# A conformer layer on one core: a new order of the blocks on all five engines and new PSUM banks, with the same instructions

## The chip, the core and the metric

The kernel runs on one core of a Trainium2 chip. A core has five engines, each with a queue of its own that it works off in order: PE (TensorE, matmuls; its weight loads are shown apart as PEld), ACT (ScalarE), DVE (VectorE), POOL (GpSimd) and SP (SyncE, which here issues DMAs). They meet at semaphores. The metric is device time in microseconds (us) of one execution, the median of the runs.

## The reference, cut to what matters

The input is 2 sequences of 4,000 tokens with 144 features, in bf16; there are 4 heads of 36 features and a convolution of 5 taps.

```python
h = _layernorm(x); x = x + 0.5 * (_silu(h @ w_ff1a) @ w_ff1b)          # 144 -> 576 -> 144
h = _layernorm(x); q, k, v = heads(h @ w_qkv)
p = _softmax(einsum('bhqd,bhkd->bhqk', q, k) * Dh ** -0.5)              # 4000 x 4000 per head
x = x + einsum('bhqk,bhkd->bhqd', p, v) @ w_o
h = _layernorm(x) @ w_pw1; h = a * _sigmoid(b)                          # a, b: its halves
c = sum(hp[:, i:i + T] * dw[i] for i in range(5)); x = x + _silu(c) @ w_pw2
h = _layernorm(x); x = x + 0.5 * (_silu(h @ w_ff2a) @ w_ff2b)
return _layernorm(x)
```

## The kernel before

Work is cut into 16 chunks of 500 tokens, 8 for each sequence (`NCH`, `CPB`, `CH`). For each chunk the first feed-forward and the projections come first (`ff1`, L1323, `pre2`, L1364; the first chunk in halves, `pre_first`, L1330), then attention, then `post1` (L1464: output projection WO, gated unit) and `post2` (L1588: convolution, second feed-forward, last normalisation, store).

Attention dominates. For a chunk of queries the keys are taken in 62 tiles of 64 and one rest of 32. Each tile gives scores of 4 heads on a 2 x 2 split of the PE array: four matmuls PS<-QT,KT of 64 x 500 (`emit_S`, L1742). The exponential goes one of two ways: on ACT, one instruction PT<-PS of 128 x 1000 over two banks (`emit_exp`, L1756), or on DVE, by four kinds of instruction on the bits of the number (`dve_tile`, L1770). Then come the products with V, PS<-PT,VA, four matmuls of 37 x 500 a tile (`o_quads`, L1806). The 37th row is the sum for the softmax. When a chunk's keys are done, `epilogue` (L1668) copies the sums out of the accumulators (QT<-PS; the QT buffer is used again for this), transposes them on PE (PS<-IDF,QT), takes reciprocals (RD) on DVE and multiplies (AN). The V products accumulate in banks 6 and 7; all other matmuls share banks 0 to 5.

Normalisations (`ln`, L1068) are statistics on DVE (ST), a power on POOL (RS), and the scaled rows XN on POOL (on DVE or ACT at the start and the end). Their transposes go through DRAM: a transpose of 32 x 32 blocks on DVE (`STREAM_TRANSPOSE`), four writes rows<-XN issued by SP, and two reads XT<-rows or XTQ<-rows (`blocks`, L994); the attention output takes the same way as AN. SP works in order: a read that waits for its writes to land holds what is behind it. Silu in the middle of the run is made from tanh (TH on ACT, then HT, U or SW on DVE), since exp and tanh need no reload of ACT's function table; at the end, behind the last exp, one table load (L2061) brings in Silu itself.

The order of the program has two layers. A scheduler (`Sched`, `pick`) records all operations once in an order that its estimated costs suggest, in blocks (steps). Then `reorder` (L279) moves the blocks of each engine by a table written out by hand or by a tool, `ORDER` (L38: "pe" from L39, "act" L70, "dve" L83, "pool" L102, "sp" L106). Each character is one block of that engine; P means stay, the characters before and behind it in `ALPHABET` (L37) mean one, two, ... places earlier or later. `PLACES` (L111) has one digit for each of the 1,724 PSUM tiles: the bank where it lies (`place`, L257); a tile of two banks takes the next one too. Both tables are only data. Dependences are kept: `reorder` finds anew which earlier tile of a bank has to be read out before a tile is written, sets the first and the last matmul of each accumulation by the new order, and `finish` (L344) works out semaphores and waits for it. `replay` (L388) emits the instructions, all from one line, L398, so the profile shows nearly everything under that line and the names of the tiles tell what it is.

Of the kernel before, what the change touches and what calls it, by code (L numbers as in the profile page):

```python
# [39 lines left out]
        "PPPPPPQOQOPPPPPRPNPPQQQQLPPQORPNPRPTMORNNVO~OLNOMrMMNPMMNNNOMNNNOPLMQMMMNNPMMNSMNLMMOOPNSOMQMSPNOPU["  # L40
        "OMNRMOPPQIRMSNPNePNOOOcNNNNNNNNNOOLbNLOOQNSH]MMOLOMPMMOOOVPNOOOOPPPTOOOTPMUQMSLNNQQNQOQQNPPPPPTPPROK"
        "PPPPPPPPPPPP`PPPQKVPPKPPMPPRPUPPPROQQQRZOQQQRRKQRRSJPRRRRRRRWSZRNYUR~NHQ@R[KEGOOOPPPPKQOPPSPPSLPQMTP"
        "PPLQQQMPPPQVPPQOX_PTOPPCRTQQRGSQIQQSQRNV8OOQNNVSNOOLOPUUNN_MMWLNNRMMMMOOOPPPPPPQQNPPRSNRSSSORRVTR[OR"
        "AKQ@PPLOOQQNPPPPPUOOOOOPQOPPPPPUOOOOQRPLU`NNNXMMPNLQMNLZRNL`MN_YLLMK`KMNLILNQJMOOOPNYOPNOOOQNNZ^NNNN"
        "OOPNQNQOYP]CNNNNOMPMSO[NKOOQNVMPMMN`NbYMMMMNOMNIcLLNL[MMMNNQNRMJQLLROQSPLRNOQOPUQOMPQMPPRPVPLQOMQNPQ"
        "QQQSKPQSQKQQQQJPPPPPWQQSPKKQQUPPPSWPQRPQAVPPPQCVPQRPWHSYPHSOPQYPQEPQCPRZUPPSOOHDPR^OKOOOOPNOOOO^NOQN"
        "NOOOSNNNNS[NNNdRMNRKYNJWJNNNNNNGOOPP^YNNNNOMNNNNRNNPPPVROOLOOPPRZNNOOOOOPNOSOPNRPSMOOPQOQWNRPRLLNSZP"
        "NPQOIOQOTPPPRPQ]P^USPMMQIQKQQ8QTQQGMRRTQQKRRRRGLRSOMRPQQQJQQRPVP[OOOQEROO^IOQLNOOPPTTOMNQ[FOQNPPSPPM"
        "HPQOQQUPLOPNVPNOOSQNLUOOPNOXPPPLTQNLMPPPQOPPTOOPTPLOOQRNOPPPQOVPNOOOORZOP[PPMOOFRZOL[ROQKQTUBOKNFPPP"
        "_OOOOOOPNOOOOWNNVNNXMNTKMNOMZQOSLNOMSPSLLTPMOOUOPNOOTQOMOPPPQOPPPQOPPPTTQOSQSSSSNEEPQOPTPTMOMORSNNOP"  # L50
        "ROYPQOPQ^NPNPQOPAOOOOOSOOOPPPQQNPPPPPPXOOOOOOOaNPPPLOOOPUMOOOO[IOOPSOOQNPHPSWOOPPPPQGPPPPQQQMPPQQNPQ"
# [12 lines left out]
        "_MORR_NPP^OHCNNNOZOWL~NHLMMNNNSOOXNOQQNSSOIVKPNPN]NOOOOOPPVOOOITNPPLPPQOWPPMRPNTKOOTNOPUMOOOQN`OOOPN"
        "OOPPPLOZOQQMPIQO^YROQQRLENO_PNPPPTQNNOROOSVO]QMNRNOPWTNOMNSOPQXbOOOQ[NO~NCdIMMMMMMMfbKMMMQMMJLMPLMUM"
        "MMNL^TR^JSLJQJUKPNLHQMPP`UNNNNOMOOOOPNOOPPPPQQNPQQQMUQQMSOPTQOPTPQUNQSPSQ<TRSSVEQQQHQQFPPPPPQSPMYTOL"
        "NNTMNNNP^[NOMNNQMMOLNN]PNOOR[OPKQN_ZLNESMOOKHOM[NPPLPNOOPPMQSTMNPQQQQRSQRRTCQVNGRNOMTTTMMNUPPQHNQSPM"
        "YVTQKLLSSOIJPSSPTMKORNOQOPPPPPPSORNSMRNRRRNQQRPFRPQQQQQQRPFQO"
    ),
    "act": (  # L70
        "PPPPPPPPPPPPPRSNNOSOOOPPPPPPPUPNOXNNOOOOOQNPPPPPPPPPROOPPQOPPPQOPPPPPPQQNPPPPPPPPPPPPPPPPPPPPPPPPPQO"
        "PPPPPPPPPPPPPPPPPPPPPPPPPPPPPPPPPPPPPPPPPPPPPPPPPPPPPPPPPPPPPPPPPPPPPPPPQOROSNOOPPPPPPPPPPPPPPPPPPPP"
        "PPPPPPPPPPPPPQOPPPPPPPPPPPPPPPPPPPPPPPPPQOPPQOPPPPPPPPPPPPPPPPPPPPPPPPPPPPPPPPPPPPPPPPPPPPPPPPPPPPPP"
        "PPPPPPPPPPPPPPPPPPPPPPPPPPPPPPPPPPPPPPPPPPPPPPPPPPPPPPPPPPPPPPPPPPPPPPPPPPPPPPPPPPPPPQOPPPPPPPPPPPPP"
        "PPPPPPPPPPPPPPPPPPPPPPPPPPPPPPQOPPQOPPPPPPPPPPPPPPPPPPPPPPPPPPPPPPPPPPPPPPPPPPPPROOPPQOPPPPPPPPPPPPP"
        "PPPPPPPPPPPPPPPPPPQOPPPPPPPPPPPPPPPPPPPPPPPPPQOQOPPPPPPPPPPPPPPPPPPPPPPPPPPPPPPPPPPPPPPPPPPPPPPPPPPP"
        "PPPPPPPPTOPNOPPPPPPPPPPPPPPPPPPPPPPPPPPPPPPPPPPPPPPPPPPPPPPPPPPPPPPPPPPQOPPPPQOPPPPPPPPPPPPPPPPPPPPP"
        "PPPPPPPPPPPPPPPPPPPPPPPPPPPPPPPPPPPPPPPROOPPQQNPPPPPPPPPPPPPPPPPPQOPPPPPPPQOPPPPPPPPPPPPPPPPPPPPPPPP"
        "PPPPPQOPPPPPPPPPPPPPPPPPROOPPPPPPPPPPPPPPPPPQOPPPPPPPPPPPPQOPPPPPPPPPPPPPPPPPPPPPPPPPPPPPPPPPPPPPPPP"
        "PQOPPPPPPPPPPPPQOPPPPPPPPPPPPPPPPPPPPPPPPPPPPPPPPPPPPPPPPPPPPPPPPPPPPPPPPPPQOPPPPPPPPPPPPPPPPPPPPPPP"  # L80
        "PPPPPPPPPPPPPPPPPPPPPPPPPPPPPPPPPQOSPNRNOQOUQNPMOPPPRORNQNPPPPPPQOROQQMPPPPPPQOPPPWORNNNOO"
    ),
# [2023 lines left out]
```

## Time and profile before

| | us |
|---|---|
| median of 3 runs | 881.04 (880.92 to 881.92) |
| span of the profiled execution | 880.5 |
| PE busy | 851.5 |
| ACT busy | 849.6 |
| DVE busy | 822.7 |
| POOL busy | 300.4 |

The profile is of one execution, taken by the hardware profiler; its own time is its span, 880.5 us, and the granted clock of TensorE is 1.00 nearly throughout. In the groups, out<-in names tiles, partitions x elements and type; then come count, busy us, mean ns of one, and after the bar the idle time of the engine just before, with what ended it. Matmuls overlap, and their ends are modelled, so a busy PE is not a PE at its peak. In a timeline, a row is start, length, engine, operation and count; in brackets stands the idle time before it and who ended it. SPq rows are DMA issues of SP.

### The profile page before, as it was taken

To read this page: it belongs to the slowest core of one execution; us is meant where nothing else is said; L and a number is where in the kernel's file an instruction comes from. 1 tells how busy PE (TensorE), PEld (TensorE's weight loads), DVE (VectorE), ACT (ScalarE), POOL (GpSimd) and SP (SyncE) were. 2 spreads that over 40 slices of the span, in tenths; PEclk is the share of its full clock that TensorE was granted. 3 is DMA by queue.
4 is the path that set the end of the run, shared out by engine and by line. 5 is a ranking of instruction groups with operands and counts; after the bars stand their busy time and mean duration, and the time that the engine had idled before them with its cause. 6 is when DMAs were issued, how large, how long until landed. Compare 5 with 4: busy or idle time off the path is not lost.

```text
span 880.5 us, 27000 instructions
## 1 busy us (share of the span) xinstructions
PE 851.5 (97%) x11419; PEld 380.2 (43%) x11419; DVE 822.7 (93%) x1812; ACT 849.6 (96%) x1098; POOL 300.4 (34%) x584
## 2 busy tenths in 40 slices
PE   8998999999999999999999999999999999999996
PEld 6543433344444443443444444344443433444366
DVE  7977999999999999999989999899999999999987
ACT  6799999999999999999999999999999999999986
POOL 7770331431336130252111813522513404032434
PEclk9999999999999999999999999999999999999999
DMA  3221001220221110212001120110110011001111
GB/s 100 44 55 38 16 18 36 62 51 16 40 49 38 23 38 22 45 24 45 16 9 30 36 44 23 23 26 20 43 31 18 21 37 20 17 12 36 27 27 33
DMA packets 114351, 28.80 MB, mean 33 GB/s; under 512 B 101090, under 2 KB 114230, under 8 KB 114230
## 3 DMA queue, kind: packets, MB, share of 16 engines
q1 hardware_dynamic: 112646, 26.39, 13.8%
q8 instruction: 89, 1.46, 0.7%
q10 hardware_dynamic: 1584, 0.69, 0.3%
q14 instruction: 32, 0.26, 0.1%
HBM read 13.44 MB, written 13.61 MB: 31 GB/s over the span
## 4 chain that ended last, share of the span: by engine, by line
ACT 46%; PE 33%; DVE 17%; POOL 2%; DMA 1%; issue 1%; SPq 1%; POOLq 0%; DVEq 0%
ACT PT L398 42%; PE PS L398 33%; DVE PT L398 7%; ACT TH L398 4%; DVE HT L398 2%; DVE ST L398 2%; DVE X L398 2%; DVE XN L398 2%; POOL RS L398 1%; POOL XN L398 1%; DVE KT L398 1%; DVE QT L398 1%; DVE AN L398 1%; SPq L398 1%; DMA rows<-XN 0%
## 5 line engine op out<-in xcount | busy, mean ns | idle before, releaser
L398 ACT ACTIVATE PT<-PS 128x1000 bf16<-128x1000 f32 (+1 forms) x818 | 757.2, 1074 | 4.1 <-PE PS L398 2.4
L398 PE MATMUL PS<-QT,KT 64*64 64x500 bf16 x3968 | 425.7, 385 | 13.0 <-ACT PT L398 5.2
L398 PE MATMUL PS<-PT,VA 64*37 64x500 bf16 x4728 | 411.5, 372 | 1.8 <-DVE QT L398 0.7
L398 DVE TENSOR_SCALAR PT<-PS 128x500 int16<-128x500 f32 x380 | 250.1, 668 | 5.8 <-PE PS L398 3.9
L398 PEld LDWEIGHTS PS<-QT,KT 64*64 64x64 bf16 x3968 | 123.4, 104 | 236.8 <-ACT PT L398 137.1
L398 POOL TENSOR_SCALAR RS<-ST 125x4 f32<-125x4 f32 x130 | 37.0, 284 | 482.2 <-DVE ST L398 475.6
L398 PEld LDWEIGHTS PS<-PT,VA 64*37 64x37 bf16 x4728 | 141.4, 96 | 96.2 <-DVE PT L398 18.7
L398 DVE TENSOR_SCALAR PT<-PT 128x1000 uint16<-128x1000 uint16 x380 | 154.5, 418 | 2.1 <-PE PS L398 0.8
L398 POOL TENSOR_SCALAR XN<-X,RS 125x144 bf16<-125x144 bf16 x260 | 150.4, 610 | 13.1 <-DMA out_dram<-XN 6.4
L398 DVE TENSOR_TENSOR PT<-PT 128x1000 bf16<-128x1000 bf16 x190 | 128.8, 679 | 1.3
L398 ACT ACTIVATE TH<-PS 128x500 bf16<-128x500 f32 (+3 forms) x194 | 107.3, 575 | 7.4 <-PE PS L398 6.5
L398 POOL TENSOR_TENSOR RS<-RS,NHALF 125x4 f32<-125x4 f32 (+1 forms) x93 | 91.7, 989 | 33.1 <-DVE RS L398 27.3
L398 DVE SCALAR_TENSOR_TENSOR HT<-TH,PS 128x500 bf16<-128x500 bf16 (+1 forms) x135 | 81.2, 615 | 12.8 <-ACT TH L398 12.0
L398 PE MATMUL PS<-XT,WA 80*128 80x500 bf16 (+5 forms) x288 | 74.5, 365 | 2.2 <-DMA XT<-rows 0.9
L398 DVE BATCH_NORM_STATS2 ST<-X 125x6 f32<-125x288 bf16 x160 | 65.7, 447 | 2.8 <-DMA X<-in_x_dram 2.7
L398 DVE SCALAR_TENSOR_TENSOR X<-PS,X 125x288 bf16<-125x288 f32 (+1 forms) x128 | 56.6, 449 | 6.5 <-PE PS L398 5.2
L398 PE MATMUL PS<-WB,HT 128*125 128x144 bf16 (+1 forms) x640 | 52.4, 230 | 0.7 <-ACT HT L398 0.5
L398 PEld LDWEIGHTS PS<-WB,HT 128*125 128x125 bf16 (+1 forms) x640 | 44.3, 136 | 14.5 <-issue 3.8
L398 PEld LDWEIGHTS PS<-XT,WA 128*128 128x128 bf16 (+1 forms) x288 | 21.2, 97 | 38.8 <-issue 10.6
L398 PE MATMUL PS<-U,DG 128*128 128x250 bf16 (+6 forms) x204 | 29.6, 264 | 0.0
L398 DVE STREAM_TRANSPOSE XN<-XN 128x320 f32<-128x320 f32 x54 | 27.0, 500 | 1.0 <-POOL XN L398 1.0
L398 POOL COPY U<-U 128x2 bf16<-128x2 bf16 (+1 forms) x54 | 9.2, 209 | 46.3 <-DVE U L398 46.3
(95 smaller groups left out, 522.6 us busy)
## 6 DMA issues: line engine op xcount, KB each, us to landing
rows<-XN SPq DMA_DIRECT2D x216, 40.0 KB, 2.0
XT<-rows SPq DMA_DIRECT2D x56, 128.0 KB, 2.0
rows<-AN SPq DMA_DIRECT2D x60, 40.0 KB, 2.0
X<-in_x_dram SPq DMA_DIRECT2D x15, 140.6 KB
XTQ<-rows SPq DMA_DIRECT2D x26, 70.3 KB
out_dram<-XN SPq DMA_DIRECT2D x13, 140.6 KB
XT<-rows SPq DMA_DIRECT2D x56, 16.0 KB, 1.9
out_dram<-XN SPq DMA_DIRECT2D x3, 70.3 KB
```

The source lines that it names most:

```text
L398: ins = getattr(eng, o.name)(*o.a, **o.k)
```

## The change

The two tables are replaced; no other line differs. Of the tables' characters:

```diff
 ORDER = {
     "pe": (
-        "PPPPPPQOQOPPPPPRPNPPQQQQLPPQORPNPRPTMORNNVO~OLNOMrMMNPMMNNNOMNNNOPLMQMMMNNPMMNSMNLMMOOPNSOMQMSPNOPU["
+        "PPPPPPPPQOPPPPQSPMOPQSQOLPQQNUOPQOLZOROMNVNuMQLxLJNSMMNNKNNNNNPQLNUJMMNOKLQRVLLILMOQOKOPPPSSPMMPTfOM"
...
     "sp": (
-        "PPPPPPPPQOPPPPPPPPPPPPPPSOTNNOOPPPQOPPPROQNPPPPPPPPPPPPPQOPPQOQOPPPPPPPPPPPPPPQOPPPPPVOPNSNNQMPPPQOP"
+        "PPPPPPPPPPPPPPPPPPPPPPPPRPRMOPPPQOPTOOOOPQOPPPPPQOPPPPPPQOPPPPPPPPPPQOQOPPPPPPQOPPPPPQOQOROOSOOOPQOP"
...
 PLACES = (
-    "4540352315301235404310523035204320244354321123203214052534114030254011540241204124012410314032034023"
+    "5103152514010310254310523035213500204345323420103501230352145130422410351241204124012410314032034023"
...
```

Counted in the two programs' orders, engine by engine (a block is what the tables move):

| engine | blocks | blocks in another place | mean shift, places | largest |
|---|---|---|---|---|
| PE | 2,855 | 2,230 | 2.6 | 26 |
| ACT | 1,093 | 125 | 0.15 | 4 |
| DVE | 1,680 | 946 | 1.05 | 17 |
| POOL | 130 | 67 | 1.2 | 12 |
| SP | 157 | 80 | 0.8 | 9 |

193 of the 1,724 PSUM tiles get another bank, 46 of them among the first 86 and 57 among the last 86.

150 lines of the change are left out of this document (75 added, 75 removed).

## The prediction, made before the changed kernel was run

> **What bounds the kernel now.** I read the page first: span, busy line and chain.
>
> ```profile
> span 880.5 us, 27000 instructions
> PE 851.5 (97%) x11419; PEld 380.2 (43%) x11419; DVE 822.7 (93%) x1812; ACT 849.6 (96%) x1098; POOL 300.4 (34%) x584
> ACT 46%; PE 33%; DVE 17%; POOL 2%; DMA 1%; issue 1%; SPq 1%; POOLq 0%; DVEq 0%
> ```
>
> Three engines are nearly full at once, and the chain passes between them. ACT is the one without choice: its instructions stay what they are, so 849.6 us is a floor, and a new order can save at most the 30.9 us in which ACT is idle. Where that idle time lies is the next view, busy time by stretch (columns: stretch, length, then busy us and count of PE, PEld, DVE, ACT, POOL; granted clock, DMA share, GB/s).
>
> ```profile
> 22.00:44.00 22.00, 20.03 (x207) 11.67 (x207) 21.02 (x55) 16.15 (x30) 16.89 (x34) 1.00 0.21 44
> 44.00:110.00 66.00, 63.28 (x868) 26.13 (x867) 53.98 (x114) 64.15 (x80) 23.23 (x44) 1.00 0.17 37
> 110.00:286.00 176.00, 172.90 (x2378) 71.72 (x2379) 171.49 (x371) 173.71 (x210) 61.47 (x113) 1.00 0.18 39
> 286.00:836.00 550.00, 538.93 (x7308) 227.50 (x7304) 523.31 (x1094) 548.38 (x680) 166.85 (x321) 1.00 0.13 27
> 836.00:858.00 22.00, 22.00 (x260) 14.21 (x257) 19.26 (x52) 19.75 (x39) 6.74 (x18) 1.00 0.13 29
> 858.00:880.50 22.50, 15.85 (x195) 13.85 (x193) 17.79 (x70) 13.56 (x35) 9.61 (x13) 0.93 0.11 33
> ```
>
> From 286 to 836 us ACT is idle 1.62 us of 550: there an order can lose, and hardly win. The rest is in the front (5.85, 1.85 and 2.29 us idle in the first three stretches) and in the end (2.25 and 8.94). From 22 to 44 it is DVE that is full (0.98 us idle). The third view is who waited for whom (us in total, times, longest).
>
> ```profile
> PEld PS L398 <- ACT PT L398: 148.3, 406, 1.1
> ACT TH L398 <- PE PS L398: 6.5, 8, 3.3
> PE PS L398 <- ACT PT L398: 6.5, 17, 0.9
> ACT XT L398 <- PE PS L398: 3.5, 6, 1.1
> ACT PT L398 <- PE PS L398: 2.4, 7, 0.6
> ```
>
> What ACT waits for is PE: a matmul that stands too far back in PE's queue. PE in turn waits for ACT to free a score bank, but mostly in the weight load (148.3 us), under matmuls that still run; the matmuls themselves stood still for it 6.5 us.
>
> **The change, part by part.** Nothing is added or removed: the two programs hold the same 15,383 recorded operations. Their orders, counted against each other:
>
> The work within PE's queue. Of the two big groups
>
> ```profile
> L398 PE MATMUL PS<-QT,KT 64*64 64x500 bf16 x3968 | 425.7, 385 | 13.0 <-ACT PT L398 5.2
> L398 PE MATMUL PS<-PT,VA 64*37 64x500 bf16 x4728 | 411.5, 372 | 1.8 <-DVE QT L398 0.7
> ```
>
> 2,346 of the 3,968 score matmuls stand earlier than before and 590 later (2.9 places earlier on the mean); the 4,728 products with V stand 3.8 places later. The first-layer feed-forward matmuls (XT,WA and XT,WE), which feed ACT's tanh, also go forward, by 2 to 6 places on the mean, and WO, GLU and the projections with them. So what ACT and DVE wait for goes ahead, and what only has to be finished some time goes back. The count of changes of tile shape on PE is 799 in both orders, so that costs nothing. What is late next: the V products, and with them the release of the 15 PT buffers; a shift of four places is one group of four matmuls, far under the time that a buffer lives, so I take nothing for it while nobody waits for a buffer (the wait rows above name none).
>
> The front, 22 to 44 us. The longest stall of ACT:
>
> ```profile
> 28.91 2.80 PE L398 MATMUL PS<-WB,HT 128*125 128x144 bf16 x40
> 31.54 1.52 PE L398 MATMUL PS<-XT,WA 128*128 128x500 bf16 x6
> 32.19 1.82 ACT L398 ACTIVATE TH<-PS 128x500 bf16<-128x500 f32 x4 [3.34 <-PE PS L398]
> ```
>
> Six XT,WA stand behind forty WB,HT. In the new order thirty stand ahead and ten behind: (31.54 - 28.91) / 40 = 66 ns each, 0.66 us for ten. One exp also moves from behind this stall to before it on ACT. But DVE has only 0.98 us to give in this stretch, so the worth lies between 0 and 0.98; I take 0.5.
>
> 44 to 110 us. Here ACT's two largest stalls end a round trip through DRAM that SP issues; this is how such a trip begins:
>
> ```profile
> 44.39 2.55 SPq L398 DMA_DIRECT2D rows<-XN  x4
> 48.35 0.81 SPq L398 DMA_DIRECT2D XT<-rows  x2
> 48.49 0.68 DVE L398 CAST KT<-PS 128x500 bf16<-128x500 f32 x1 [0.99 <-PE PS L398]
> 49.09 0.41 DVE L398 SCALAR_TENSOR_TENSOR HT<-TH,PS 128x250 bf16<-128x250 bf16 x1
> 49.41 0.51 DVE L398 STREAM_TRANSPOSE XN<-XN 128x320 f32<-128x320 f32 x1
> 49.95 5.39 SPq L398 DMA_DIRECT2D rows<-XN  x8
> 54.65 1.57 PE L398 MATMUL PS<-XT,WA 128*128 128x500 bf16 x5
> 70.39 1.07 ACT L398 ACTIVATE TH<-PS 128x500 bf16<-128x500 f32 x2 [0.69 <-PE PS L398]
> 73.86 1.90 ACT L398 ACTIVATE PT<-PS 128x1000 bf16<-128x1000 f32 x2 [0.61 <-PE PS L398]
> ```
>
> SP stands from 44.39 + 2.55 = 46.94 to 48.35 for the landing of its own writes before it issues the read XT<-rows; the next writes then wait for DVE's transpose. In the new order the transpose stands ahead of the CAST (which waited 0.99), and four writes ahead of the read; over the whole queue 15 pairs of read and write are exchanged this way and one the other way. DVE is free at 48.49 - 0.99 = 47.50; with HT (0.41) and the transpose (0.51) the writes can start at 48.4. They and what follows them come up to 49.95 - 48.4 = 1.5 us sooner, the read 48.4 + 2.55 - 48.35 = 2.6 later. The read was issued by 48.35 + 0.81 = 49.16, lands 2.0 later (the row below) at 51.2, and its user on PE starts at 54.65: 3.5 us spare hide the 2.6. If the transpose comes no sooner, that cover is gone: read at 49.95 + 2.55 = 52.5, landing at 55.3, 0.7 late. Between -0.7 and the 1.85 us of ACT's idle time in this stretch I take 0.9, half of it.
>
> ```profile
> XT<-rows SPq DMA_DIRECT2D x56, 128.0 KB, 2.0
> ```
>
> 110 to 836 us. ACT's idle time is 2.29 + 1.62 = 3.91 us. POOL's order changes most here: normalisations are issued sooner (one is moved six blocks forward), copies of the convolution's halo later.
>
> ```profile
> L398 POOL TENSOR_SCALAR RS<-ST 125x4 f32<-125x4 f32 x130 | 37.0, 284 | 482.2 <-DVE ST L398 475.6
> L398 POOL TENSOR_SCALAR XN<-X,RS 125x144 bf16<-125x144 bf16 x260 | 150.4, 610 | 13.1 <-DMA out_dram<-XN 6.4
> L398 POOL TENSOR_TENSOR RS<-RS,NHALF 125x4 f32<-125x4 f32 (+1 forms) x93 | 91.7, 989 | 33.1 <-DVE RS L398 27.3
> ```
>
> POOL is busy 61.47 + 166.85 of 726 us and mostly waits for DVE, so I cost it at nothing. If that cover fails, a halo copy that now stands behind one normalisation comes 2 x 0.284 + 0.989 + 4 x 0.610 = 4.0 us later, and its convolution's matmuls hold all of PE behind them. For the feeders that go forward I take about a quarter of the 3.91: 1.1, from 0 to 3.9.
>
> The end.
>
> ```profile
> 825.71 26.55 PE PS L398 x328
> 844.74 1.09 ACT L398 ACTIVATE TH<-PS 128x500 bf16<-128x500 f32 x2
> 845.38 0.68 DVE L398 SCALAR_TENSOR_TENSOR HT<-TH,PS 128x500 bf16<-128x500 bf16 x1 [2.16 <-ACT TH L398]
> 845.85 1.28 ACT L398 ACT_TABLE_LOAD   x1
> 847.25 0.57 ACT L398 ACTIVATE TH<-PS 128x500 bf16<-128x500 f32 x1
> 847.72 0.58 ACT L398 ACTIVATE QT<-PS 128x500 f32<-128x500 f32 x1
> 848.18 0.59 ACT L398 ACTIVATE TH<-PS 128x500 bf16<-128x500 f32 x1
> ```
>
> The table load and the small instruction behind it hold ACT from 845.85 to 847.25, 1.40 us, ahead of the copy QT<-PS, which carries half of the last attention block to its transposes. In the new order that copy and both tanh stand before the load. The last exp goes back behind two tanh, 2 x (847.72 - 847.25) = 0.94 us, and delays the other side of the same block; PE moves the block's last products and its transposes two to three groups forward, and DVE its reciprocal and AN ahead of two HT of 0.68 us. Between -0.94 and 1.40 for the copy, I take 1.0, since the rest of the block's path is shortened too.
>
> The banks. 193 of 1,724 tiles get another place. Tiles whose bank was used by one of the last three tiles grow from 408 to 444, 36 more. Each is at worst a mean wait of the row PEld <- ACT PT, 148.3 / 406 = 0.365 us, so 13.1 us; at best the matmuls' own share, 6.5 / 406 = 16 ns, so 0.6. I take 0.6, because PE's matmuls are idle only 11.07 us between 286 and 836, which is nearer to the second. [...]
>
> Sum: 0.5 + 0.9 + 1.1 + 1.0 - 0.6 = 2.9 us. 880.5 - 2.9 = 877.6 of its own time; the median of the runs shown, 881.04, is 0.54 above the profiled span, so **878.1**.
>
> **The rivals.**
> (a) A larger gain. All of ACT's idle time of 44 to 286 (4.14), DVE's 0.98 and ACT's 2.25 of 836 to 858 go: 7.4 us, 873.7. For it: the order takes up the start and the end most thoroughly (46 and 57 of 86 tiles in the first and the last twentieth get another bank). Against: a chain that changes engines does not close every hole.
> (b) Nothing. PE reaches the score tiles sooner and only waits there for the bank that ACT frees; the wait moves from ACT's column to PE's. 881.0, give or take 1.7. For it: the 406 waits. Against: the front and the end wait for PE, not for banks.
> (c) Slower, by PE held at banks. PE issues in order; where a score matmul that went forward stands for its bank, all that follows stands too, the feeders of tanh among it. It decides where the added standing is more than PE's spare time (0.44 us in 22 us between 286 and 836), since nothing there can be won back. At half of the upper price of the 36 reuses, 6.6 us: 887.6. For it: the middle has no reserve. Against: tanh's feeders went forward too.
> (d) The change does not do what it says. The operations are the same one by one, so I give this nothing.
>
> **How the numbers follow.** Under 0.2%, 1.8 us, is about what a measurement of this kernel cannot tell from no change. Forecast: 0.50, its own range 874.5 to 879.2 (the terms at their upper and at their lower halves). (a) 0.14, (b) 0.14, (c) 0.22. The range takes (a) with the middle's 1.62 us added, 872, and (c) nearly whole, 887; outside are some 0.15. Faster by over 0.2% (under 879.3): 0.64; within: 0.14; slower: 0.22.
>
> **What would show it.** ACT's idle time from 44 to 286 falls under 3 us; the stall of 3.34 is at least 0.6 shorter; SP's four writes near 50 us start at least 1 us sooner, and the read behind them is late for nobody; the copy QT<-PS of the end is done before the table load, and the span after it is no longer than 880.5 - 845.85 = 34.65 less 1. PE <- ACT PT stays under 10 us. Against it: more than 3 us of ACT idle between 286 and 836, or PE <- ACT PT in the tens, which is (c); a span after the load that grew, which is the delayed last exp.

## The result, and the profile after

The changed kernel took 883.5 us (median of 21 runs, 881.67 to 886.17), the kernel before 881.55 beside it (21 runs, 880.43 to 882.45): ratio 1.0021 [1.0014, 1.0027], 1.9 us slower where 2.9 us less was forecast. In each of its 21 runs the time is the span plus 1.8 us. So the profiled execution of before, with its span of 880.5, took about 882.3, not the 880.5 that the section on the profile gives as its own time: it was itself among the slower ones. One execution of before, beside the last two experiments, ran at a mean clock of 0.557 and took 1289.38 us; it is left out of every count and comparison below.

The page of the changed kernel, its span, busy line and chain:

```profile
span 882.4 us, 27009 instructions
PE 847.2 (96%) x11419; PEld 382.4 (43%) x11419; DVE 822.0 (93%) x1812; ACT 850.3 (96%) x1098; POOL 302.0 (34%) x584
ACT 50%; PE 23%; DVE 18%; DMA 3%; SPq 2%; POOL 1%; issue 1%; ACTq 0%; DVEq 0%; POOLq 0%
```

ACT has 0.7 us more of busy time and is idle 32.1 us instead of 30.9. In the chain PE gave up 10 points, and DMA and SP's queue together went from 2% to 5%: the end is now reached more often through round trips through DRAM. The same stretches as in the prediction, busy time by stretch:

```profile
22.00:44.00 22.00, 20.25 (x179) 11.05 (x176) 19.71 (x52) 14.89 (x28) 14.63 (x29) 0.92 0.21 44
44.00:110.00 66.00, 63.59 (x895) 26.73 (x894) 56.27 (x120) 64.91 (x82) 25.09 (x47) 1.00 0.17 37
110.00:286.00 176.00, 171.64 (x2372) 72.03 (x2368) 169.65 (x369) 173.26 (x209) 62.82 (x111) 1.00 0.18 38
286.00:836.00 550.00, 534.45 (x7302) 229.75 (x7298) 521.04 (x1091) 547.70 (x680) 163.40 (x317) 1.00 0.12 27
836.00:858.00 22.00, 21.75 (x258) 13.19 (x259) 19.10 (x49) 19.67 (x34) 10.25 (x25) 1.00 0.17 38
858.00:882.40 24.40, 17.78 (x217) 15.59 (x214) 19.48 (x76) 15.42 (x41) 9.55 (x13) 0.93 0.10 31
```

ACT's idle time by stretch, before and after: 5.85 and 7.11, 1.85 and 1.09, 2.29 and 2.74, 1.62 and 2.30, 2.25 and 2.33, 8.94 and 8.98. Only 44 to 110 gained. The first row shows a granted clock of 0.92, where before has 1.00. Last the waits (us, times, longest):

```profile
PE PS L398 <- ACT PT L398: 10.1, 32, 0.6
ACT TH L398 <- PE PS L398: 7.5, 13, 1.2
```

PE's own standing for ACT grew from 6.5 to 10.1 us, and ACT waits for tanh's matmuls 13 times instead of 8, with a longest wait of 1.2 us instead of 3.3.

One tool used below is the lag: the start of ACT's k-th instruction less the start of the k-th in the profile of before. Both kernels issue the same number, so it shows where time is lost or won. For the changed kernel it is +0.52 at 38 us of before's time, +1.99 at 65, +0.22 at 96, -0.91 at 198, +0.85 at 264, +0.35 at 524, +1.36 at 816 and +1.90 at the end. It falls to +0.22 partly because the profile of before loses about 1 us near 73 us by a long DMA issue (told further down), which the profile of e16, with the same order there, does not have.

### The profile page after: what moved, and what is told of

It reads as the page before. It is cut to its first block, busy times and chain, and to the rows that moved or that the text cites. A ratio compares the mean times of both kernels' runs of the same rounds, so it can differ in the third digit from the quotient of the medians.

```text
span 882.4 us, 27009 instructions
## 1 busy us (share of the span) xinstructions
PE 847.2 (96%) x11419; PEld 382.4 (43%) x11419; DVE 822.0 (93%) x1812; ACT 850.3 (96%) x1098; POOL 302.0 (34%) x584
## 4 chain that ended last, share of the span: by engine, by line
ACT 50%; PE 23%; DVE 18%; DMA 3%; SPq 2%; POOL 1%; issue 1%; ACTq 0%; DVEq 0%; POOLq 0%
ACT PT L398 46%; PE PS L398 23%; DVE PT L398 8%; ACT TH L398 5%; SPq L398 2%; DVE HT L398 2%; DVE ST L398 2%; DVE X L398 2%; DVE XN L398 1%; DMA XT<-rows 1%; POOL XN L398 1%; DMA XTQ<-rows 1%; DVE QT L398 1%; DMA rows<-XN 1%; POOL RS L398 1%
## 5 line engine op out<-in xcount | busy, mean ns | idle before, releaser
L398 PE MATMUL PS<-QT,KT 64*64 64x500 bf16 x3968 | 420.9, 384 | 16.4 <-ACT PT L398 9.6
L398 PE MATMUL PS<-PT,VA 64*37 64x500 bf16 x4728 | 402.6, 372 | 0.7 <-DVE QT L398 0.4
L398 ACT ACTIVATE TH<-PS 128x500 bf16<-128x500 f32 (+3 forms) x194 | 104.8, 560 | 8.2 <-PE PS L398 7.5
L398 PEld LDWEIGHTS PS<-XT,WA 128*128 128x128 bf16 (+1 forms) x288 | 21.2, 97 | 37.3 <-issue 10.1
```

The source lines that it names most:

```text
L398: ins = getattr(eng, o.name)(*o.a, **o.k)
```

## The experiments

Every kernel here computes the whole reference; only orders, banks and, in four of them, spare matmuls that nobody reads differ. Each ratio is to before, measured beside it on the same chip, with its 95% interval. "Mean clock 0.996 or less" is counted over the executions of a kernel; half a clock for 3.4 us in 882 takes 0.002 from the mean. The experiments were measured in five sessions, and the changed kernel's own ratio was 1.0021 in the first measurement and 1.0035 in a later session (e9); a difference of some 0.0014 between kernels of different sessions is therefore no proof by itself.

### First round: which part of the change costs?

**e1_front_before**: the changed kernel, but all blocks up to 100 us in before's order, and 52 tiles in before's banks (186 blocks of PE, 36 of ACT, 91 of DVE, 5 of POOL, 2 of SP).

```diff
     "pe": (
-        "PPPPPPPPQOPPPPQSPMOPQSQOLPQQNUOPQOLZOROMNVNuMQLxLJNSMMNNKNNNNNPQLNUJMMNOKLQRVLLILMOQOKOPPPSSPMMPTfOM"
+        "PPPPPPQOQOPPPPPRPNPPQQQQLPPQORPNPRPTMORNNVO~OLNOMrMMNPMMNNNOMNNNOPLMQMMMNNPMMNSMNLMMOOPNSOMQMSPNOPU["
...
```

> The changed kernel (883.5 us), but all engines in the order and the banks of before up to 100 us. Theory S (late transfers: SP's queue puts writes of a later step ahead of reads and of writes that PE waits for, and PE, ACT and DVE stand together behind them): the front holds one such stall of the changed profile, ACT 0.63 us at 57 us, and what had been won elsewhere in the front is lost again; 883.0, between 882.6 and 883.5. Rival C (clock: the granted clock of 0.52 and 0.63 at 22 to 26 us in the profile of the changed kernel is what costs): no stretch ahead of 100 us below 1.00, and at least 1.2 us faster, 882.3 or less. Rival M (the loss is spread over the middle, from matmuls held at banks): 883.5, nothing changes.

Measured 882.66 beside 881.46, 1.0013 [1.0004, 1.0022]; no execution of 11 has a mean clock of 0.996 or less. That is inside theory S's range, and more than the 882.3 that rival C allowed. What is left of the change behind 100 us is still slower than before.

**e2_end_before**: before's order and banks from 838 us on (78 blocks of PE, 20 ACT, 75 DVE, 6 POOL, 6 SP, 57 tiles).

```diff
     "act": (
...
-        "PPPPPPPPPPPPPPPPPPPPPPPPPPPPPPPPPPQRSORKNQORRNQMPPPPPPRORNOQQQMPQOROQQMPPPPPPQOPPPWORNNNOO"
+        "PPPPPPPPPPPPPPPPPPPPPPPPPPPPPPPPPQOSPNRNOQOUQNPMOPPPRORNQNPPPPPPQOROQQMPPPPPPQOPPPWORNNNOOPPP"
...
```

> The changed kernel, but from 838 us on in the order and the banks of before, the table load ahead of the copy QT<-PS among it. Theory S: the end is no part of the loss; the lag of 1.42 us that the profile of the changed kernel has at 842 us stays; 883.0 to 883.5. Rival E (the later table load holds the gated unit's Silu SW, and with it the last feed-forward): the 0.5 us by which the lag grows from 842 us to the end goes, 883.0 or less. The prediction's own term (the copy ahead of the load is worth 1.0 us): the run is 1.0 slower than the changed kernel, 884.5.

Measured 882.23, 1.0012 [1.0002, 1.0022]. That agrees with rival E and not with the prediction's term, by which it should have been 1.0 us slower than the changed kernel; but the two intervals overlap, so a gain is not shown.

**e3_sp_before**: SP's queue as before (66 of its 80 moved blocks go back; the last stores keep their new place).

```diff
     "sp": (
-        "PPPPPPPPPPPPPPPPPPPPPPPPRPRMOPPPQOPTOOOOPQOPPPPPQOPPPPPPQOPPPPPPPPPPQOQOPPPPPPQOPPPPPQOQOROOSOOOPQOP"
-        "TOPNOPPQOPPPPZOOOOOOOVNNNOOQNROOPPPPPPPPYOOOOOOOPNPPPQO"
+        "PPPPPPPPQOPPPPPPPPPPPPPPSOTNNOOPPPQOPPPROQNPPPPPPPPPPPPPQOPPQOQOPPPPPPPPPPPPPPQOPPPPPVOPNSNNQMPPPQOP"
+        "ROYNOOOPNOOUNTNOMNPPPVOOOOOQNPPPPPPPPPQOYOOOOOOOPNPPPPPPP"
```

> The changed kernel, but SP's queue in the order of before wherever the other engines' orders allow it: 66 of the 80 moved blocks go back (all up to 545 us), the stretches at 680 to 720 and 800 to 850 us stay. Theory S: the stalls behind reads at 57, 232 and 247 us (ACT 0.63, 0.88 and 0.36 us) go, 1.9 us at most; 881.9, between 881.5 and 882.6. Rival M: the matmuls still stand at banks, 883.3 to 883.7. Rival N (the other engines' new order needs SP's new order): slower than the changed kernel, 884 or more.

Measured 881.52, 0.9998 [0.9989, 1.0007]: the whole loss is gone with SP's order alone, 0.0023 less than the changed kernel, and the two intervals are apart. The clock does not make this difference: among the executions with a mean clock over 0.996, the changed kernel is 1.2 us above before on the mean (12 runs), and e3 0.1 us below it (10 runs). The place where it shows best, first the timeline of the changed kernel (start, length, engine, operation, idle time before and its releaser):

```profile
218.97 2.60 SPq L398 DMA_DIRECT2D rows<-AN  x4
220.61 0.49 DVE L398 STREAM_TRANSPOSE XN<-XN 128x320 f32<-128x320 f32 x1
...
223.70 2.56 SPq L398 DMA_DIRECT2D rows<-XN  x4
227.67 1.67 SPq L398 DMA_DIRECT2D XTQ<-rows  x2
232.21 0.59 PE L398 MATMUL PS<-XTQ,WK 72*128 72x500 bf16 x2 [0.96 <-DMA XTQ<-rows]
233.19 1.00 ACT L398 ACTIVATE PT<-PS 128x1000 bf16<-128x1000 f32 x1 [0.88 <-PE PS L398]
```

and that of e3:

```profile
219.22 0.49 DVE L398 STREAM_TRANSPOSE XN<-XN 128x320 f32<-128x320 f32 x1
219.74 2.89 SPq L398 DMA_DIRECT2D rows<-XN  x4
224.04 1.67 SPq L398 DMA_DIRECT2D XTQ<-rows  x2
225.75 2.60 SPq L398 DMA_DIRECT2D rows<-AN  x4
229.79 0.59 PE L398 MATMUL PS<-XTQ,WK 72*128 72x500 bf16 x2
```

With before's queue the writes start 0.03 us behind the transpose (219.22 + 0.49 = 219.71). In the new queue the four writes of AN, and behind them a read that nobody wants yet, stand ahead of them: the transpose is done at 221.10, its writes start at 223.70, 2.6 us later, the read of XTQ follows them, and PE stands 0.96 us for it, then ACT 0.88. e1, which has this stretch of the new queue too, shows the same wait of ACT there (0.83 us at 232.01). It is not in every execution: in the profiles of e2 and e15, with this queue as well, the writes start 2.0 to 2.2 us behind their transpose, and nobody stands. There the read ahead of them takes 1.65 and 1.07 us to issue, here 2.05. The new order uses up the spare time, and a long issue then decides.

**e4_banks_before**: the new order with 188 of the 193 tiles back in before's banks.

```diff
 PLACES = (
-    "5103152514010310254310523035213500204345323420103501230352145130422410351241204124012410314032034023"
+    "4540352315301235404310523035204320244354321123203214052534114030254011540241204124012410314032034023"
...
```

> The changed kernel, but 188 of the 193 tiles that changed their bank lie where they lay before (the other 5 cannot with this order); the order of all engines is that of the change. Tiles whose bank was used by one of the last three tiles: 434 against 444. Theory S: nothing, 883.0 to 884.0. Rival M (banks): PE <- ACT PT falls from 10.1 us towards the 6.5 of before, and the time by up to 3.6 us, 880 to 882. Rival N (the new banks were what the new order needs): slower, 884.5 or more.

Measured 906.91, 1.0296 [1.0274, 1.0318]. Reuses of a bank within three tiles are 434, against the change's 444, so their number can't be the price. Eight of the 25 us are lost by 45 us. From 44 to 110 us its mean granted clock is 0.95, where the changed kernel has 1.00. By `reorder`, a tile waits for the reader of whatever stood in its bank, and the new order has moved those readers; which tiles these are was not followed up. What the run shows is that the new order without its banks is far worse than either kernel.

### Second round: SP's queue, its places, and the table load

**e5_after_sp_in_before**: before with the new SP queue (73 of the 80 moved blocks).

```diff
     "sp": (
-        "PPPPPPPPQOPPPPPPPPPPPPPPSOTNNOOPPPQOPPPROQNPPPPPPPPPPPPPQOPPQOQOPPPPPPPPPPPPPPQOPPPPPVOPNSNNQMPPPQOP"
-        "ROYNOOOPNOOUNTNOMNPPPSOOOPPPPPPPPPPPPPQOQOPPPPQQN"
+        "PPPPPPPPPPPPPPPPPPPPPPPPRPRMOPPPQOPTOOOOPQOPPPPPQOPPPPPPQOPPPPPPPPPPQOQOPPPPPPQOPPPPPVOPNSNNSMOOPQOP"
+        "TOPNOPPQOPPPPZOOOOOOOVNNNOOQNROOPPPPPPPPYOOOOOOOPNPPPQOPP"
```

> The kernel before (881.46 us beside the first four runs), with SP's queue alone in the new order, as far as the other engines' old orders allow it: 73 of the 80 moved blocks; the seven at 470 to 500 us stay. Theory S: SP's order is what costs, on whatever order of the other engines; the 2.0 us that its undoing gave (883.5 to 881.52) come back as a loss, 882.8 to 884.0, with PE <- DMA XTQ<-rows in the waits near 225 us. Rival N (only the pair of the new orders of SP and of the other engines costs): 881.0 to 882.0.

Measured 897.77 beside 882.0, 1.0175 [1.0161, 1.0189], for another reason than the one expected. The timeline of e5:

```profile
569.52 0.27 SPq L398 DMA_DIRECT2D out_dram<-XN  x1
569.84 2.55 SPq L398 DMA_DIRECT2D rows<-XN  x4
573.80 0.83 SPq L398 DMA_DIRECT2D XT<-rows  x2
576.45 1.01 PE L398 MATMUL PS<-XT,WA 128*128 128x500 bf16 x2 [11.34 <-DMA XT<-rows]
577.50 0.59 ACT L398 ACTIVATE TH<-PS 128x500 bf16<-128x500 f32 x1 [11.75 <-PE PS L398]
```

A store that the new queue issues earlier waits at the head of SP for an XN that before's order makes later. SP issues nothing from 560 us at the latest to 569.52, and with it stands a round trip that does not depend on the store. One stall of 11.75 us is most of the 15.8. Behind it PE is slow as well: two matmuls PS<-XT,WA take 1.01 us at 576.45, against 0.63 at 564.51 in the profile of before, and four PS<-PT,VA 0.63 at 577.82, against 0.38 at 565.30. The mean granted clock of this execution is 0.990, that of before 0.998. The lag grows there from 12.3 to 13.7 us; the rest is 0.5 us ahead of the stall and 1.9 behind it. So this run says what a queue in order costs, but not what the new queue costs beside the new order.

**e6_two_places**: the changed kernel with SP as before only near 50 us and from 182 to 230 us (10 positions).

```diff
     "sp": (
-        "PPPPPPPPPPPPPPPPPPPPPPPPRPRMOPPPQOPTOOOOPQOPPPPPQOPPPPPPQOPPPPPPPPPPQOQOPPPPPPQOPPPPPQOQOROOSOOOPQOP"
+        "PPPPPPPPQOPPPPPPPPPPPPPPRPRMOPPPQOQOPPPROQNPPPPPQOPPPPPPQOPPPPPPPPPPQOQOPPPPPPQOPPPPPQOQOROOSOOOPQOP"
...
```

> The changed kernel (883.5 us), SP's queue back in the old order at two places only: at 50 us (read XT<-rows ahead of four writes) and at 182 to 230 us (six blocks: the four writes rows<-AN and the read XT<-rows that the change put ahead of rows<-XN go behind them again). Theory S: these two hold the stalls of 0.63 and 0.88 us and most of the 2.0 us; 881.7 to 882.4. Rival D (the cost is spread over all of the 20 places where SP's order differs): a tenth of the 2.0 us, 883.0 to 883.6.

Measured 883.17, 1.0008 [1.0000, 1.0017]: 0.0013 less than the changed kernel, about half of what the whole queue brings. That lies between theory S (most of it) and rival D (a tenth), and the interval overlaps that of the changed kernel, so the two places' share is not shown closely.

**e7_sp_and_end_before**: e2 and e3 together.

```diff
     "act": (
...
-        "PPPPPPPPPPPPPPPPPPPPPPPPPPPPPPPPPPQRSORKNQORRNQMPPPPPPRORNOQQQMPQOROQQMPPPPPPQOPPPWORNNNOO"
+        "PPPPPPPPPPPPPPPPPPPPPPPPPPPPPPPPPQOSPNRNOQOUQNPMOPPPRORNQNPPPPPPQOROQQMPPPPPPQOPPPWORNNNOOPPP"
...
     "sp": (
...
-        "TOPNOPPQOPPPPZOOOOOOOVNNNOOQNROOPPPPPPPPYOOOOOOOPNPPPQO"
+        "ROYNOOOPNOOUNTNOMNPPPVOOOOOQNPPPPPPPPPQOVOOOOOOQOPPPPPPPP"
```

> The changed kernel with SP's queue of before (881.52 us) and all engines in the order and the banks of before from 838 us on. If the end of the change costs what the run with only the end of before won (883.5 - 882.23 = 1.3 us, or 0.6 by the two profiles' lag at 838 us and at the end): 880.2 to 880.9, faster than both kernels. If the two gains are one and the same: 881.5.

Measured 881.73, 1.0001 [0.9992, 1.0009], the same as e3: with before's SP queue the end brings nothing more.

**e8_load_early**: e3, with the table load and its small instruction right behind the last exp again (4 blocks of ACT).

```diff
     "act": (
...
-        "PPPPPPPPPPPPPPPPPPPPPPPPPPPPPPPPPPQRSORKNQORRNQMPPPPPPRORNOQQQMPQOROQQMPPPPPPQOPPPWORNNNOOPPP"
+        "PPPPPPPPPPPPPPPPPPPPPPPPPPPPPPPPPPQSPPRKOQORRNQMPPPPPPRORNOQQQMPQOROQQMPPPPPPQOPPPWORNNNOOPPP"
```

> The changed kernel with SP's queue of before (881.52 us), and ACT's table load and its small instruction moved back: right behind the last exp, ahead of the last two tanh and the copy QT<-PS, as before. The prediction's term (the copy ahead of the load is worth 1.0 us): slower by about 1.0, 882.5. Rival E (the load's place decides when the Silu of the gated unit, SW, can start, and that is the path to the end; SW lagged 0.55 us more than ACT did at 843 us): faster by 0.4 to 0.6, 881.0. If neither path is alone: within 0.4 of 881.5.

Measured 882.98, 1.0011 [1.0002, 1.0020], so 0.0013 or 1.1 us more than e3; the two intervals overlap a little. In the profiles the lag from 816 us to the end grows by 1.30 in e8 (-0.26 to +1.04) and by 0.49 in e3 (-1.25 to -0.76), 0.81 more. The timeline of e8:

```profile
845.67 1.28 ACT L398 ACT_TABLE_LOAD   x1
...
847.54 0.58 ACT L398 ACTIVATE QT<-PS 128x500 f32<-128x500 f32 x1
...
849.66 0.90 ACT L398 ACTIVATE SW<-PS 128x500 bf16<-128x500 f32 x2 [1.07 <-PE PS L398]
```

The load delays the copy, and ACT then stands 1.07 us for PE. The profiles' 0.8 and the runs' 1.1 us are near the term of 1.0 for the copy, seen by itself; the runs alone would not prove it.

### Third round: one stretch alone in the kernel before

**e9_changed_again**: the changed kernel once more, with no edit.

> The changed kernel as it is, once more, beside the three others on one chip. Ratio to before as at first, 1.0014 to 1.0027; a granted clock of 0.996 or less over the whole run in a third of the executions (25 of 76 so far with the change's front, none of 65 with the front of before).

Measured 885.44 beside 882.08, 1.0035 [1.0023, 1.0046], of 6 runs, above the range that was expected; 4 of the 6 have a mean clock of 0.996 or less.

**e10_front_alone**: before with the new order and banks up to 40 us (35 blocks of PE, 48 DVE, 19 ACT, 5 POOL, none of SP, 37 tiles).

```diff
     "pe": (
-        "PPPPPPQOQOPPPPPRPNPPQQQQLPPQORPNPRPTMORNNVO~OLNOMrMMNPMMNNNOMNNNOPLMQMMMNNPMMNSMNLMMOOPNSOMQMSPNOPU["
+        "PPPPPPPPQOPPPPQSPMOPQSQOLPQQNUOPQOLZOROMNVN~OLMQLrLJNSMMNNKNNNNNPQLNQJMMNNPMMNSMNLMMOOPNSOMQMSPNOPU["
...
```

> The kernel before, but up to 40 us in the order and the banks of the change (35 blocks of PE, 48 of DVE, 19 of ACT stand elsewhere, SP's queue untouched, 37 tiles in another bank). Theory C (this front leaves PE idle longer at 18 to 22 us, 2.59 us busy of 4.00 against 3.07, and that now and then drops the granted clock at 22 to 26 us to 0.57; such runs are 1.4 us longer): three or four of 11 runs with a clock of 0.996 or less over the whole run, and the median 0.2 to 1.2 us over before. The prediction's front term (0.5 us won by the earlier XT,WA): 0.5 faster, no run at 0.996.

Measured 884.55, 1.0026 [1.0015, 1.0038]; 5 of 6 runs have a mean clock of 0.996 or less, and the profiled one shows 0.57 from 22 to 26 us. The front by itself is slower than before.

**e11_middle_alone** and **e12_middle_long**: before with the new order and banks from 100 to 262 us (384 blocks of PE, 157 DVE, 12 ACT, 15 POOL, none of SP, 23 tiles), and from 100 to 838 us, with SP's queue of before up to 670 us.

```diff
     "dve": (
...
-        "PPPPPPPSOOOPPQOPPPPPPPPPPPPPPPPQOQOPPPPPPROQQMQOQOPPQORSQMQQQQQRPQWQRPQLPQQQVQQQSUKTQ2KMPQQQRRORPQQR"
+        "PPPPPPPSOOOPPQOPPPPPPPPPPPPPPPPQOQOPPPPPPROQQMQOQOPPQORSQMQQQQQRPQVQRPQLQRPQTQQRRRKVR2OPLRRRSSPRRRRR"
...
```

> The kernel before, with the change's order of PE (384 blocks), DVE (157), ACT (12) and POOL (15) and its 23 banks from 100 to 262 us alone; SP's queue, front and end of before. Theory S says that the order of PE, DVE and ACT was a gain once SP's is out of it: the profiles lag less by 1.1 us between 100 and 200 us in five runs alike; 1.1 us faster than before, between 0.6 and 1.4, and faster than both kernels. Rival M (no order wins in a stretch that full): same as before within 0.4.

> As the run before this, but with the change's order from 100 to 838 us (SP's queue of before up to 670 us, its changed places at 680 to 850 us stay). If the drift of 0.9 us that the runs with the change's order show between 280 and 840 us belongs to that order: 0.1 to 0.5 us faster than before, so slower than the run with 100 to 262 us. If the drift was chance: as that run, 1.1 faster.

Measured 881.1, 0.9991 [0.9982, 1.0000], and 882.08, 0.9997 [0.9988, 1.0006]. No execution of either has a low clock. The order from 100 to 262 wins, by an interval that ends at 1.0000. That it is given back behind 262 us is not shown by the runs, whose intervals overlap, but the profiles agree with it: from 524 to 816 us the lag grows by 0.89 us in e12 and by 0.05 in e11. And with SP's queue of before, the new order of the other engines from 100 to 838 us costs nothing, where e1, with the new queue behind 100 us, was slower than before.

### Fourth round: the clock

The windows that put the clock under suspicion, from the stretch of 3.4 us ahead of the low clock and the stretch of it (length, busy PE, PEld, DVE, ACT, POOL, then granted clock). Before:

```profile
18.60:22.00 3.40, 2.47 (x38) 0.90 (x35) 3.38 (x10) 3.40 (x7) 3.22 (x8) 1.00 0.29 59
22.00:25.40 3.40, 3.22 (x34) 1.08 (x34) 2.96 (x9) 3.40 (x5) 3.07 (x8) 1.00 0.16 29
```

The changed kernel:

```profile
18.60:22.00 3.40, 1.99 (x22) 0.72 (x22) 3.40 (x7) 3.21 (x4) 3.25 (x8) 1.00 0.09 18
22.00:25.40 3.40, 3.40 (x24) 0.89 (x20) 2.64 (x9) 2.03 (x4) 3.22 (x8) 0.51 0.23 41
```

e3, with the same front:

```profile
18.60:22.00 3.40, 1.98 (x29) 0.63 (x23) 3.23 (x7) 3.19 (x6) 3.23 (x8) 1.00 0.19 42
22.00:25.40 3.40, 3.36 (x36) 1.18 (x36) 3.40 (x11) 2.86 (x4) 3.14 (x8) 1.00 0.16 29
```

Before, PE is busy 2.47 of 3.40 us (73%) and keeps its clock of 1.00. In the new front it is busy 1.99 (58%), and in this execution the clock is then 0.51 for 3.4 us: 24 matmuls are recorded in a time in which before has 34, and ACT stands 1.37 us. In e3's execution the same share is followed by a full clock, so it strikes some executions and not others.

Where these profiles show a low clock at 22 us, it lasts 3.4 us. In the changed kernel it is 0.50 from 22.08 to 25.49 us. In the profile of e2 it is 0.54, 0.50, 0.50 and 0.76 in the four microseconds from 22 us on, which makes 3.40 us at half; in e10 and e14 it is 0.57 on the mean from 22 to 26, which makes 3.44.

What stands ahead of it is alike: from 18.60 to 22.00 us PE is busy 1.99 us in the changed kernel, 2.00 in e10 and 1.98 in e14, and from 19 to 22 us 1.59 of 3.00 in e2. With 2.47 us in before and 2.99 in e13 and e15 (told further down) the clock from 22.00 to 25.40 is 1.00. But e3 has 1.98 us as well, and 1.00 behind it. So ahead of each of these drops PE had little to do, and not every such stretch brings one; what else decides, no run shows.

Counted: with the new front and its own banks, and no spare matmuls, 37 of 93 executions have a mean clock of 0.996 or less; with before's order there none of 44 (e1, e11, e12, e16) and none of the 124 of before beside them. The count is rough, since the mean does not say where the clock fell: in the profile of e18 (told further down; a mean of 0.996) it is 0.82 from 15 to 16 us and 0.50 from 16 to 19, behind two microseconds, from 13 to 15, with PE busy 0.36 and 0.64. In the 21 runs of the changed kernel the 9 with a low mean take 884.09 on the mean, the 12 others 882.69: 1.4 us, near the 1.7 that half a clock for 3.4 us takes from PE. A single execution need not show it: the profiled one of e2 has the same drop and is, with 880.92 us, the fastest of its 11.

**e13_front_filled**: e10 with 15 spare matmuls in PE's gaps, 6 and 9 of them (in its profile at 20.3 and 21.1 us; 128 x 128, into banks that are free there, read by nobody).

```diff
+    spare = []
+    for at, bk, n in ((357, 2, 6), (372, 0, 9)):
+        R.tiles.append((bk,))
+        for j in range(n):
...
+            o.name, o.a = "matmul", (PSV[:, bk, j % 4 * 128:j % 4 * 128 + 128],)
+            o.k = dict(lhsT=IDENT[:, :], rhs=IDENT[:, :], start=True, stop=True)
...
+        R.ops.insert(at + 1, o)
     R.reorder(ORDER)
```

> The kernel before with the change's order and banks up to 40 us (as the run of the front alone, 1.0026), and 15 spare matmuls PS<-IDENT of 128x128 on PE at 19.7 to 21.3 us, in free banks, while PE would stand: busy at 18 to 22 us 3.2 to 3.5 us instead of 2.60. They add work and speed nothing up by themselves. Theory C (clock): no run with a clock of 0.996 or less, no stretch at 22 to 26 us below 1.00, and the 1.6 us by which the two fronts of the change differ with and without the drop come back: 1.0000 to 1.0015. Rival O (the order of the front itself costs): as the front alone, 1.0015 to 1.0035, or more by the spare work.

**e14_front_again**: e10 once more beside it.

> The front alone once more, beside the filled one on the same chip: 1.0015 to 1.0038, with a clock of 0.996 or less in a third to all of the runs.

e13 took 883.36 beside 881.63, 1.0019 [1.0010, 1.0029], with 1 of 11 runs at a low clock; e14 885.73, 1.0041 [1.0027, 1.0054], with 3 of 5. So the spare matmuls bring most of the clock's share back, but 1.0019 lies in rival O's range: this front's order costs as well. Windows of e13, and the row of its timeline that tells where it is still slow:

```profile
18.60:22.00 3.40, 2.99 (x33) 1.46 (x33) 3.38 (x6) 3.19 (x5) 3.19 (x8) 1.00 0.12 24
22.00:25.40 3.40, 3.36 (x35) 1.14 (x34) 3.40 (x11) 2.87 (x5) 3.22 (x7) 1.00 0.18 30
```

```profile
41.44 0.58 ACT L398 ACTIVATE XTQ<-PS 72x500 bf16<-72x500 bf16 x1 [2.55 <-PE PS L398]
```

Busy for 88%, PE keeps its clock of 1.00 in this execution. The 2.55 us stand where the new order ends and before's begins: the second of the three XTQ copies waits 0.33 us in before, 1.91 in the changed kernel and in e15, and 2.53 to 2.55 in e10, e13 and e14. So these three pay some 0.6 us for the seam as well, and their ratio is not the price of the front inside the changed kernel.

**e15_changed_filled**: the changed kernel with the same 15 spare matmuls.

> The changed kernel with the same 15 spare matmuls, nothing else altered. Theory C: the clock's share goes, SP's share stays: 1.0005 to 1.0015 instead of 1.0021 and 1.0035. Rival O: as the changed kernel, 1.0020 to 1.0040.

Measured 881.12, 0.9992 [0.9983, 1.0000]: no run of 11 at a low clock, and 0.0029 (2.6 us) less than the changed kernel, for 15 matmuls more. That is below theory C's range (1.0005 to 1.0015): the clock's share alone does not explain so much.

**e16_middle_again**: e11 once more.

> The change's order from 100 to 262 us alone, once more, for a closer interval: 0.9991 at first; 0.9982 to 1.0000, faster than before.

Measured 880.82, 0.9989 [0.9981, 0.9998], the fastest here by its ratio: before, with the new order from 100 to 262 us.

### Fifth round: a control, and the shares together

**e17_before_filled**: before with 6 spare matmuls at the same place (bank 4).

```diff
+    for at, bk, n in ((361, 4, 6),):
...
```

> The kernel before with spare matmuls of the same kind in its own gap at the same place: six PS<-IDENT at 19.65 to 20.05 us (the gap holds no more, and no bank is free in the next). Theory C: this front never drops its clock, so they win nothing; 0.9993 to 1.0008. Rival W (spare matmuls help by themselves, whatever the clock): 0.9970 to 0.9985, as they helped the changed kernel by 0.0029 (1.0021 to 0.9992).

Measured 881.99 beside 881.57, 1.0012 [0.9999, 1.0024]: spare matmuls as such win nothing. Two of its 11 runs have a lower mean clock, 0.992 (885.23 and 885.74 us); in which stretch was not profiled.

**e18_filled_sp_end**: e15 with SP's queue and the end as before.

```diff
     "sp": (
...
-        "TOPNOPPQOPPPPZOOOOOOOVNNNOOQNROOPPPPPPPPYOOOOOOOPNPPPQO"
+        "ROYNOOOPNOOUNTNOMNPPPVOOOOOQNPPPPPPPPPQOVOOOOOOQOPPPPPPPP"
```

> The changed kernel with the 15 spare matmuls, SP's queue of before and the end of before (all engines, from 838 us). If the shares add (clock 0.0029; SP 0.0023, by 1.0021 to 0.9998; end 0.0009, by 1.0021 to 1.0012): 0.9960. If SP's share and the clock's are mostly the same runs (late reads matter where the front came late): 0.9980 to 0.9992. Slower than the changed kernel filled (0.9992) if the parts need each other.

Measured 880.57, 0.9993 [0.9984, 1.0002]: no better than e15. Each repair alone takes the loss away (SP 0.0023, the spare matmuls 0.0029), and both together not twice. They are not terms of a sum.

## Why the prediction was wrong

**The offset.** The sum was made against a span whose time was taken to be 0.54 us below the median; it was 1.8 us below its own time. The forecast span of 877.6 would have been 879.4 us. That is 1.3 of the miss of 5.4 us (883.5 against 878.1), and no mechanism.

**The front, 0.5: wrong in sign.** The stall of 3.34 us did shrink by 2.15 us, as the moved WB,HT said, but the idle time only moved. The timeline of the changed kernel:

```profile
32.70 1.54 ACT L398 ACTIVATE TH<-PS 128x500 bf16<-128x500 f32 x3 [1.19 <-PE PS L398]
36.31 2.48 ACT L398 ACTIVATE TH<-PS 128x250 bf16<-128x250 f32 x5 [1.03 <-PE PS L398]
41.79 0.58 ACT L398 ACTIVATE XTQ<-PS 72x500 bf16<-72x500 bf16 x1 [1.91 <-PE PS L398]
```

ACT's gaps over 0.25 us from 22 to 44 sum to 5.74 before, 6.76 in the changed kernel, and 5.81 in e3, which has the same order and kept its clock. So the order won nothing here, and the clock took about 1 us of this profile. The step that failed is "the worth lies between 0 and 0.98": a front that gives PE less to do between 18.6 and 22 us can lose, and the clock, 1.00 in every row of before there, was not looked at as something that the order sets. The runs put the loss in place of the 0.5: e13, whose clock mostly stays full, is still 0.0019 slower than before, of which the seam explains about 0.0007.

**44 to 110, 0.9: the cover failed.** The prediction had 3.5 us of spare time hide the read's 2.6. The changed kernel:

```profile
45.92 8.11 SPq L398 DMA_DIRECT2D rows<-XN  x8
54.08 1.07 SPq L398 DMA_DIRECT2D XT<-rows  x2
56.63 1.54 PE L398 MATMUL PS<-XT,WA 128*128 128x500 bf16 x6 [0.51 <-DMA XT<-rows]
57.30 1.06 ACT L398 ACTIVATE TH<-PS 128x500 bf16<-128x500 f32 x2 [0.63 <-PE PS L398]
```

Eight writes stand ahead of the read, and one of them took 1.93 us to issue instead of 0.62 (50.79 to 52.72). The read is issued at 54.08, not at 51, and PE and ACT wait for it. The last four of the eight were to start at 48.4 and start at 50.17, no sooner than the 49.95 of before: DVE's transpose did move forward against the one ahead of it (4.26 us behind it instead of 5.54), but that one came at 45.39 instead of 43.87, since the front was late. With the long write that makes the 3.1 us. How long the eight writes take differs: 8.11 us here, 7.39 in e15 and 7.24 in e2, with the same queue. In these two the read is issued at 52.83 and 53.34, and ACT does not stand here. So the new order leaves the round trip without spare time, and chance decides whether it is late. The other half of the term, ACT's stall of 0.61 at 73.86, was chance too, in the profile of before. Its cause there:

```profile
65.99 2.30 SPq L398 DMA_DIRECT2D XT<-rows  x2
...
72.88 0.59 PE L398 MATMUL PS<-XTQ,WK 72*128 72x500 bf16 x2 [0.90 <-DMA XTQ<-rows]
```

and the same read in e16, whose order there is before's:

```profile
65.70 1.08 SPq L398 DMA_DIRECT2D XT<-rows  x2
```

2.30 and 1.08 us, and in e16 no stall follows. The idle time of 44 to 110 did fall, by 0.76, but much of that is an accident that one profile had and the other had not. From 44 to 286 it is 3.83 us, where the prediction named less than 3 as its sign.

**SP's other exchanges: not priced.** Fifteen pairs of read and write were counted, and one was worked out. The one that cost most is that of 219 to 233 us, shown with e3. The step that failed is the cover: it was tested at one place, and at none for what stands behind a write that waits, or behind a long issue, so that all others went into the sum at nothing. In its place the runs show 2.0 us, by which the changed kernel gets faster when SP's queue alone is put back (e3).

**110 to 836, 1.1: about right up to 262 us by the ratios, then given back.** (A quarter of the 3.91 would be 0.98.) The windows of e16, with the new order of this stretch in the kernel before:

```profile
110.00:286.00 176.00, 173.14 (x2393) 72.27 (x2390) 170.96 (x370) 174.03 (x211) 63.56 (x115) 1.00 0.18 38
```

ACT is idle 1.97 us there instead of 2.29, and 1.64 in e11; by the ratios the stretch wins 0.8 and 1.0 us, about the term. The profiles show less, 0.3 and 0.65 us of ACT's idle time, and the intervals of the ratios end at 1.0000 and 0.9998. All this is with SP's queue of before. e12 gives it back behind 262: 286 to 836 is where the prediction said that an order can lose and hardly win, and in the changed kernel ACT's idle time there grew from 1.62 to 2.30. POOL, costed at nothing, has no stall in any of this.

**The end, 1.0: the term right, its neighbour missed.** The changed kernel:

```profile
847.87 0.59 ACT L398 ACTIVATE QT<-PS 128x500 f32<-128x500 f32 x1
849.21 1.28 ACT L398 ACT_TABLE_LOAD   x1
...
851.01 0.48 SPq L398 DMA_DIRECT2D out_dram<-XN  x1
854.66 0.90 ACT L398 ACTIVATE XN<-X,RS 125x144 bf16<-125x144 bf16 x2 [0.77 <-DMA out_dram<-XN]
```

The copy is done before the load, 0.15 us later than before while ACT as a whole is 1.42 late: 1.27 won, and e8 agrees by undoing it. But from 816 us to the end the lag still grew, from 1.36 to 1.90, so the rest of the new end loses more than the copy wins. SP now issues the store of an XN at 851.01 instead of 799.67, and that buffer's next user on ACT waits 0.77 us for it; but the store is not the loss, for in e3, which issues it at 848.71, the same instruction waits 0.65 us for DVE instead. The SW instructions stand behind the later load; whether that is the path, no run shows. The mark named for this step (the span behind the load under 33.65) is met, with 882.4 - 849.21 = 33.19, and says nothing, since three instructions that stood behind the load now stand ahead of it. It should have been a lag.

**The banks, -0.6, and rival (c).** PE <- ACT PT ended at 10.1 us, 3.6 more, at the edge of the mark of 10. Rival (c) made that the cause of a slower kernel. The waits of e15:

```profile
PE PS L398 <- ACT PT L398: 9.5, 31, 0.6
```

The same standing is in kernels that are no slower than before, e15, e3 (10.0 us) and e12 (10.4): (c) falls as the cause, though its sign was right and its price of 6.6 too high. Rival (a) fell too. By size rival (b), nothing, came nearest, but not by its reason.

**What the loss of 1.9 is.** Low clock in 9 of 21 runs at 1.4 us gives 0.6 us on the mean. SP's queue alone back brings 2.0; two of its places 1.1 and the end back 0.8, which the runs can't tell from nothing. The middle's gain of at most 1 stands against these. The shares overlap: e3 and e15 each take the whole loss away, and e18 with both repairs is no better. Two things stay open. The 12 runs of the changed kernel without a low clock take 882.69, e15's 881.2 on the mean: the spare matmuls bring 1.5 us beyond the clock, and no run shows how; part may be what one kernel differs by between sessions. And e3 has a low clock in 1 of 11 runs, where the same front has 9 of 21 in the changed kernel, which may be chance.

## What to carry to other kernels

Before an engine's queue is reordered, list for each DMA queue in order what stands ahead of each read that feeds PE, writes and stores that may wait for their data included, and price all such places, not one. Look in a new order for stretches where PE has less to do than before (here 1.99 of 3.40 us instead of 2.47), and take the granted clock from several executions, since one may miss it. Before a stall of the old profile is counted as a gain, look for it in a second execution, and set the profiled execution's time against its span from runs that show both.

## What the runs showed of the hardware that was not expected

- The granted clock fell to half for 3.4 us in some executions and not in others of the same order. Where a profile shows it at 22 us (the changed kernel, e2, e10, e14), PE had been busy for only five to six tenths of the time ahead (1.98 to 2.00 us of 3.40; in e2 1.59 of the last 3.00); in e3 the clock stayed at 1.00 behind the same 1.98 us. In 37 of 93 executions with the new front the mean clock is low; with the gaps filled, in 2 of 33, and in the one of these that was profiled (e18) it fell ahead of the filled gaps, 0.50 from 16 to 19 us.
- DMA issues on SP have long ones among them: in the profile of before 34 of 466 took over 0.25 us longer than the median of their kind (same destination and source), 22 us in all, in the changed kernel 26 and 19 us. The median of rows<-XN is 0.62 us in both, the longest 1.55 and 1.93; of XT<-rows 0.43, the longest 1.66 and 1.58. How long one and the same pair of reads takes changes: the XT<-rows behind the writes of AN near 221 us took 2.05 us in the changed kernel, 1.65 in e2 and 1.07 in e15. Where a round trip has little to spare, a long one is met as a stall: of these three, only the changed kernel's ACT stands, 0.88 us at 233.19.
- 15 matmuls that compute nothing made the changed kernel 2.6 us faster; 6 in the kernel before made it no faster.
